# A decode-attention and FFN kernel: moving the FFN weight loads forward in the load stream, and reworking the last stage

## The chip, the cores and the metric

The kernel runs on one core of one Trainium2 chip. The metric is device microseconds per execution. A quoted time is the median of several runs; almost all runs of one kernel lie within 0.1% of that median. A profile is of one execution, whose span is some 2 us shorter than its measured time, because the span runs from the first to the last instruction. The program uses one core.

Engines: PE is TensorE (PEld its weight loads), DVE is VectorE, ACT is ScalarE, SP (SPq in the profile) is the sync engine, which issues nearly all loads.

## The reference

```python
x = A_x                                          # 2 x 1 x 512
q = layernorm(x) @ wq                            # 32 heads of 128, one query token per batch
scores = q k^T / sqrt(128)                       # k_cache: 2 x 32 x 8192 x 128, bf16
h  = x + (softmax(scores) @ v_cache) @ wo        # v_cache: the same size
y  = layernorm(h)
h2 = h + (relu(y @ W_gate) * (y @ W_up)) @ W_down   # 512 -> 1376 -> 512
```

Nearly all of the work is reading the two caches, 268 MB. A "pair" below is two heads of one batch: one K tile and one V tile of 4 MB each; there are 32 pairs. The weights wq, wo and the three FFN matrices are another 12.6 MB.

## The kernel before

Four buffers of 4 MB rotate: K of even pairs in 0, K of odd pairs in 2, V in 1 and 3. K[p+2] is issued when pair p has been read, V[p+2] when the P.V matmuls of pair p are done. VectorE computes three quarters of a pair's scores as a product and a tree of additions, in two halves; TensorE transposes and multiplies the rest:

```python
for c in range(NCH):                    # two halves, 48 of the 128 tiles each
    dve.wait(t_k[p])
    dve: prod = k_t[:, half, :] * q     # L324
    dve: four halving additions         # L332
    dve: scores = reduce(prod)          # L339
    if c == 0: ... TensorE: transposes and scores of the last 32 tiles; exp of those ...
    act: exp(scores)
    if last_pair and c == 0:
        t_O[3] = normalize(3, 24, 31, t_batch[3], False)   # pairs 24 to 30
```

At the end the FFN weights go into the buffer of K30, which has to be read first; the last V is issued after them, in four pieces:

```python
if p == NP - 2:                                   # pair 30
    sp.wait(*t_kfree[p])
    ... W_gate, W_up, W_down[0:1280] ("(r p) n -> p r n": rows of 1 KB) into slot[s] ...
    nc.sync.dma_start(wd_last[0:FR, :], B_W_down[1280:F]).then_inc(sem_w, 16)   # L384
...
if p == NP - 2:
    sp.wait(t_vlast)
    for ci, (j0, j1) in enumerate(((0, 48), (48, 96), (96, 112), (112, 128))):
        nc.sync.dma_start(slot[sl][:, ...], src[:, ...]).then_inc(sem_vl[ci], 16)   # L426
```

So the stream ends K30, V30, K31, weights, V31. Then come the output projection of the last pairs, the residual `hb`, and the FFN:

```python
pe.wait(t_O[3]); o_proj(range(24, 30), 0, 2); o_proj(range(30, 32), 0, 1)   # 32 matmuls
... o_scale; o_proj(range(30, 32), 1, 2) ...                                # 8 matmuls
hb = Wp + x
d_b = hb - mean;  d2 = d_b * d_b;  memset(Op[1]); memset(Sp[1])
t_u = ffn_in(Sp[1], wup);  t_g = ffn_in(Op[1], wgt)                  # 44 matmuls each
for c in range(DC): matmul(Sp[0][:, 64:66], lhsT=ones_f, rhs=d2[...])   # fp32 norm sums
hd = max(gate, 0) * up;  down projection (44 matmuls);  out = y * (1/var) + hb
```

The softmax here doesn't subtract the row's maximum and nothing guards it: scores larger than these inputs give would overflow.

## Time and profile before

Before: 683.12 us (682.39 to 683.75, 3 runs), span 680.7 us.

| What | Value | View |
|---|---|---|
| bytes moved | 281.97 MB | page, DMA queues |
| rate in most slices | 428 to 431 GB/s | page, slices |
| one pair on VectorE | 15.5 us | timeline, from K30's landing at 626.39 to 641.85 |
| K30 to K31 landing (8.4 MB) | 19.44 us | timeline |
| `hb` ready | 669.80 us | chain of waits |

The page's slices of the kernel before: one row per engine or quantity, 40 equal slices of 17 us, counted here from 0; the digits are tenths of busy time.

```profile
DVE  1777778867777887777782788776777886777781
DMA  9999999999999999999999999999999999999990
GB/s 374 437 432 431 428 428 430 430 429 430 432 429 431 430 429 429 430 430 429 430 345 435 429 428 428 428 430 431 428 429 430 429 429 430 430 429 430 409 360 27
```

The load engines are busy throughout, so the stream is the limit. VectorE is about three quarters busy: it keeps up, with idle time of about 4 us per pair. The dip to 345 (slice 20) is wo, in rows of 1 KB; the last three slices are the end of the stream.

The chain of waits of the kernel before, its end; columns are start, duration (us), and what it was.

```profile
639.48 11.62 SPq L384
651.10 0.05 issue
...
652.56 15.23 DMA slot<-in_A_v_cache_dram
667.79 0.05 issue
667.84 0.59 PE O L407 x16
668.42 1.35 PE W L303 x40
...
669.80 0.18 DVE hb L447
...
670.95 1.52 PE S L473 x44
672.47 1.39 PE O L473 x44
673.86 1.71 PE S L482 x8
675.56 1.47 PE O L501 x44
```

Here a load ends the stream: the last piece of V31 lands at 667.79, TensorE does 16 matmuls with it, then 40 of the output projection, then up, gate, the norm sums (L482, 8 records in fp32) and down, one after the other. The first line says that the sync engine was held for 11.62 us in issuing 96 rows of W_down; only then could the last V be issued. Stretches of 2 us at that place show a slower stream (the last two columns are DMA share and GB/s):

```profile
648.00:650.00 2.00, 2.00 (x31) 2.00 (x32) 1.97 (x2) 1.57 (x2) 0.00 (x0) 0.50 0.98 368
650.00:652.00 2.00, 1.07 (x19) 0.64 (x17) 1.94 (x2) 1.49 (x3) 0.00 (x0) 0.50 0.49 193
652.00:654.00 2.00, 0.00 (x0) 0.00 (x0) 1.86 (x6) 1.05 (x7) 0.00 (x0) 0.50 0.88 284
```

VectorE's two halves of pair 31 ended with this line in the timeline of the kernel before (start, duration, engine, line, operation), at 661.88, six microseconds before the last load landed:

```profile
661.33 0.55 DVE L339 TENSOR_REDUCE scores<-prod 128x48 f32<-128x384 bf16 x1
```

### The profile page before, as it was taken

To read this page: it belongs to the slowest core of one execution; us is meant where nothing else is said; L and a number is where in the kernel's file an instruction comes from. 1 tells how busy PE (TensorE), PEld (TensorE's weight loads), DVE (VectorE), ACT (ScalarE), POOL (GpSimd) and SP (SyncE) were. 2 spreads that over 40 slices of the span, in tenths; PEclk is the share of its full clock that TensorE was granted. 3 is DMA by queue.
4 is the path that set the end of the run, shared out by engine and by line. 5 is a ranking of instruction groups with operands and counts; after the bars stand their busy time and mean duration, and the time that the engine had idled before them with its cause. 6 is when DMAs were issued, how large, how long until landed. Compare 5 with 4: busy or idle time off the path is not lost.

```text
span 680.7 us, 14440 instructions
## 1 busy us (share of the span) xinstructions
PE 297.6 (44%) x6602; PEld 268.7 (39%) x6602; DVE 492.9 (72%) x426; ACT 202.6 (30%) x523; POOL 1.8 (0%) x11
## 2 busy tenths in 40 slices
PE   2544334444543445354342344535443444653436
PEld 2444334443433334344341333434433443543326
DVE  1777778867777887777782788776777886777781
ACT  0632223333222333332131233333222333332230
POOL 1000000000000000000000000000000000000000
PEclk9955566555555555655555556555556555555555
DMA  9999999999999999999999999999999999999990
GB/s 374 437 432 431 428 428 430 430 429 430 432 429 431 430 429 429 430 430 429 430 345 435 429 428 428 428 430 431 428 429 430 429 429 430 430 429 430 409 360 27
DMA packets 15936, 281.97 MB, mean 414 GB/s; under 512 B 1442, under 2 KB 6916, under 8 KB 7172
## 3 DMA queue, kind: packets, MB, share of 16 engines
q1 hardware_dynamic: 15872, 281.06, 97.1%
q8 instruction: 51, 0.84, 0.5%
q14 instruction: 9, 0.07, 0.0%
q10 hardware_dynamic: 4, 0.00, 0.0%
HBM read 281.05 MB, written 0.00 MB: 413 GB/s over the span
## 4 chain that ended last, share of the span: by engine, by line
DMA 69%; DVE 27%; SPq 2%; PE 1%; issue 1%; DVEq 0%
DMA slot<-in_A_k_cache_dram 66%; DVE prod L324 16%; DVE tb L332 6%; DVE prod L332 3%; DMA slot<-in_A_v_cache_dram 2%; SPq L384 2%; DVE scores L339 1%; PE S L482 0%; PE S L473 0%; PE O L501 0%; PE O L473 0%; PE W L303 0%; SPq L426 0%; SPq L133 0%; SPq L379 0%
## 5 line engine op out<-in xcount | busy, mean ns | idle before, releaser
L324 DVE TENSOR_TENSOR prod<-slot,q_b 128x6144 bf16<-128x6144 bf16 x64 | 214.9, 3358 | 135.3 <-DMA slot<-in_A_k_cache_dram 134.2
L407 PE MATMUL O<-e,slot 128*128 128x2 bf16 x4096 | 119.5, 165 | 248.4 <-ACT e L261 124.2
L407 PEld LDWEIGHTS O<-e,slot 128*128 128x128 bf16 x4096 | 114.4, 104 | 253.6 <-DMA slot<-in_A_v_cache_dram 126.9
L355 ACT ACTIVATE kT<-T 128x1024 bf16<-128x1024 bf16 x128 | 126.9, 1022 | 171.7 <-PE T L349 170.7
L349 PE MATMUL T<-ident,slot 128*128 128x128 bf16 x1024 | 123.6, 307 | 71.9 <-DMA slot<-in_A_k_cache_dram 71.9
L332 DVE TENSOR_TENSOR tb<-prod 128x3072 bf16<-128x3072 bf16 (+1 forms) x128 | 148.2, 1158 | 4.4
L349 PEld LDWEIGHTS T<-ident,slot 128*128 128x128 bf16 x1024 | 100.3, 141 | 74.9 <-DMA slot<-in_A_k_cache_dram 74.9
L261 ACT ACTIVATE e<-scores 64x48 bf16<-64x48 f32 x128 | 32.8, 256 | 255.0 <-DVE scores L339 253.4
L332 DVE TENSOR_TENSOR prod<-tb 128x1536 bf16<-128x1536 bf16 (+1 forms) x128 | 84.2, 658 | 4.4
L253 PE MATMUL S<-qT,kT 128*128 128x2 bf16 x1024 | 48.4, 168 | 33.0 <-ACT kT L355 31.7
L253 PEld LDWEIGHTS S<-qT,kT 128*128 128x128 bf16 x1024 | 41.1, 107 | 52.0 <-ACT kT L355 52.0
L339 DVE TENSOR_REDUCE scores<-prod 128x48 f32<-128x384 bf16 x64 | 35.4, 553 | 2.2
L261 ACT ACTIVATION_READ_ACCUMULATOR e<-scores 64x1 f32 x128 | 23.7, 185 | 0.0
L261 ACT ACTIVATE e<-S 64x32 bf16<-64x32 f32 x64 | 13.0, 204 | 15.1 <-PE S L253 14.3
L261 ACT ACTIVATION_READ_ACCUMULATOR e<-S 64x1 f32 x64 | 12.9, 201 | 0.7
L235 ACT ACTIVATE q_b<-O 128x512 bf16<-128x512 f32 x8 | 4.3, 594 | 15.6 <-PE O L230 15.6
L208 DVE CAST qT<-W 128x64 bf16<-128x64 f32 x1 | 0.2, 225 | 12.0 <-PE W L203 12.0
L203 PE MATMUL W<-xlT,slot 128*128 128x2 bf16 x128 | 3.6, 165 | 8.6 <-DMA slot<-in_A_wq_dram 8.6
L203 PEld LDWEIGHTS W<-xlT,slot 128*128 128x128 bf16 x128 | 3.5, 104 | 8.7 <-DMA slot<-in_A_wq_dram 8.7
L279 DVE TENSOR_REDUCE zr<-O 128x16 f32<-128x48 f32 (+1 forms) x4 | 0.8, 204 | 8.3 <-PE O L271 8.3
L271 PE MATMUL S<-zs,ones_f 128*128 128x6 f32 x2 | 0.6, 367 | 10.9 <-ACT e L261 10.9
L230 PE MATMUL O<-ident,qrep 128*128 128x128 bf16 x32 | 4.3, 303 | 1.7 <-ACT q_b L235 0.9
(56 smaller groups left out, 47.2 us busy)
## 6 DMA issues: line engine op xcount, KB each, us to landing
slot<-in_A_k_cache_dram SPq DMA_DIRECT2D x32, 4096.0 KB, 27.9
slot<-in_A_v_cache_dram SPq DMA_DIRECT2D x31, 4096.0 KB, 32.1
slot<-in_A_wq_dram SPq DMA_DIRECT2D x1, 4096.0 KB, 12.3
wo_sb<-in_A_wo_dram SPq DMA_DIRECT2D x1, 4096.0 KB, 43.4
slot<-in_A_v_cache_dram SPq DMA_DIRECT2D x2, 1536.0 KB, 12.1
slot<-in_B_W_gate_dram SPq DMA_DIRECT2D x1, 1376.0 KB, 10.0
slot<-in_B_W_up_dram SPq DMA_DIRECT2D x1, 1376.0 KB, 13.2
slot<-in_B_W_down_dram SPq DMA_DIRECT2D x1, 1280.0 KB, 15.0
```

The lines of the kernel that those rows point to most:

```text
L203: i = nc.tensor.matmul(Wp[:, h * B:(h + 1) * B], lhsT=wq[:, c, h * Dh:(h + 1) * Dh], rhs=lT[:, c * B:(c + 1) * B], start=(c == 0), stop=(c ...
L230: i = nc.tensor.matmul(Op[m % 2][:, k * 128:(k + 1) * 128], lhsT=qrep[m % 2][:, k * 128:(k + 1) * 128], rhs=ident[:], start=True, stop=True)
L235: t_cp[m] = act.run(nc.scalar.activation(out=q_b[:, m * 512:(m + 1) * 512], in_=Op[m % 2][:], func=ACT.Copy))
L253: i = nc.tensor.matmul(Sp[p % 2][:, 2 * jj:2 * jj + 2], lhsT=kT[n % 3][:, k * 128:(k + 1) * 128], rhs=qT[:, 2 * p:2 * p + 2], start=True, ...
L261: t = act.run(nc.scalar.activation(out=e_t[p % 2][q, j0:j0 + nj, a], in_=src(q, a), func=ACT.Exp, scale=inv_sqrt_dh, accum_out=zs[q, 2 * p ...
L324: t_dm = dve.run(nc.vector.tensor_tensor(out=prod[:], in0=k_t[:, c * JC:(c + 1) * JC, :], in1=qv, op=ALU.mult))
L332: dve.run(nc.vector.tensor_tensor(out=o, in0=cur[:, :, 0:half], in1=cur[:, :, half:w], op=ALU.add))
L339: t_s = dve.run(nc.vector.tensor_reduce(out=sc[:], in_=cur, axis=AX.X, op=ALU.add))
L349: i = nc.tensor.transpose(Tp[n % 3][:, k * 128:(k + 1) * 128], k_t[:, j, :], ident[:])
L355: t_ev[n] = act.run(nc.scalar.activation(out=kT[n % 3][:], in_=Tp[n % 3][:], func=ACT.Copy))
L384: nc.sync.dma_start(wd_last[0:FR, :], B_W_down[1280:F]).then_inc(sem_w, 16)
L407: i = nc.tensor.matmul(Op[k % 2][:, col:col + 2], lhsT=v_t[:, j, :], rhs=e_t[p % 2][:, j, :], start=(nmm == 0), stop=(nmm == J - 1))
```

## The change

The intent: give the FFN weights a home that doesn't depend on K30 (the buffer of wq, then of wo), so that they can be loaded early; let the stream end in V alone; shorten the last stage. Cut to its core:

```diff
+        X = sb("X", [128, XW + FC * D], BF16)          # wq, then wo, then the FFN weights
+                t_v[1] = load(3, slot[3][:], kv(A_v_cache, 1))
                 sp.wait(t_q)
-                t_v[1] = load(3, slot[3][:], kv(A_v_cache, 1))
+                ... wo heads 0-23 into X, heads 24-31 into wo_t (before: wo behind pair 14) ...
@@ main loop
-                        if last_pair and c == 0:
-                            t_O[3] = normalize(3, 24, 31, t_batch[3], False)
...
+                    if p < NP - 2:
+                        pv(p)
+                        if p == W_AT:                               # W_AT = 24 (before: 27)
+                            t_om = pe.run(o_proj(range(0, HM), 0, 2))
+                        if p < NP - 4:
+                            load_v(p + 2)
+                        elif p == NP - 3:                           # K31 was issued just above
+                            load_v(p + 1)
+                            load_v(p + 2, vparts)                   # last piece 8 tiles, was 16
+                        if p == W_AT + 2:                           # pair 26
+                            sp.wait(t_om)
+                            ... W_gate, W_up, W_down into X ...
@@ after the loop
+                pv(NP - 2)
+                t_O[3] = normalize(3, 24, 31, t_batch[3], False)
                 pe.wait(t_O[3])
-                o_proj(range(24, 30), 0, 2)
+                o_proj(range(HM, 30), 0, 2)
                 o_proj(range(30, 32), 0, 1)
+                normalize(4, 31, 32, z_sum(4, 31, 32), True)
+                pv(NP - 1)
@@ FFN
-                ... d2, two memsets, then up, gate, four fp32 matmuls for the norm sums ...
+                t_u = ffn_in(Sp[1], wup, 0, FC)
+                t_g = (ffn_in(Op[1], wgt, 0, FH), ffn_in(Wp, wgt, FH, FC))
+                ... d2, its sum over c, split into two bf16 parts vh on VectorE ...
+                for k in range(2):
+                    i = nc.tensor.matmul(Sp[0][:, 64:64 + B], lhsT=onesn[:], rhs=vh[:, k * B:(k + 1) * B], ...)
+                ... down in two halves, each after its half of hd ...
```

The stream now ends: K28, V28, weights, K29, V29, K30, K31, V30, V31.

## The prediction

> **What bounds it now.** The load stream. The page's slice table shows the DMA busy 9 tenths in 39 of 40 slices at 428-431 GB/s; 281.97 MB at 430 is 656 us of the 680.7 us span. The Trainium skill ("DMA: Bandwidth & Descriptors", Specifications) gives 435 GB/s as the fabric ceiling; the trace agrees, so only losses can be won. The timeline by line shows wo running at about 335 GB/s (it costs some 3 us over full rate). At the end, the issue of the last 96 rows of W_down blocks the sync queue for 11.62 us (639.5 to 651.1), so the last V (651.1) starts late: the stretches 650-654 move 193 and 284 GB/s. The last V lands at 667.8; 12.9 us of tail follow.
>
> **The step that decides.** The change moves the weights ahead of K29, and K31 ahead of V30. Same bytes, so the stream still ends at 666-668. The blocking issue moves too: K29 queues behind W_down's rows as the last V did, so I expect the bubble again, near 604. But the stream's last three transfers are now K31, V30, V31, and VectorE becomes the tail. From the timeline: one pair costs VectorE 15.5 us, one 4 MB transfer takes 9.85 us. K30 landed at 626.4; with 4.2 MB of weights ahead (10.8 us at the measured rates, up to 12 with the bubble) it lands at 637-638.5. VectorE then does pairs 30 and 31 without a pause: 31.0 us, to 668-669.5. Before, pair 31 was done at 661.9.
>
> Everything after that is serial in the new order, since the batch-3 normalisation now sits behind pair 31 on VectorE and the last P.V behind z_sum on PE: normalise 0.75, 32 output-projection matmuls 1.15, z_sum 0.5, 128 P.V matmuls 3.66 (28.6 ns each), scale and the last 8 matmuls 0.8. So the residual (hb) is ready at about 675.0-676.6 instead of 669.8: +5.2 to +6.8 us. Halving the last chunk gains nothing; V31 has landed when PE asks.
>
> **Gains in the tail, on the path.** The fp32 norm matmuls (8 records, 1.71 us on the chain) become two bf16 ones of 0.2; they fill the wait for the product, and the down projection starts as soon as the gate ends: -1.5 us. The two memsets and the square leave the path: -0.3. Total -1.8.
>
> **Off the path.** wo moves from pair 14 to the start, same rows and rate; K2 lands some 12.5 us later and pair 18 when it did. It blocks the sync queue there, the stream staying full. 96 projection matmuls move from pair 27 to 24, under the loads.
>
> **Sum.** +6.0 - 1.8 is about +4: **687.0 us**, 8 in 10 between 683.0 and 691.0. Faster by over 2%: 0.01; within 2%: 0.97; slower by over 2%: 0.02.
>
> **What would show it.** Chain of waits: right, if it ends through VectorE's work on pair 31 (pairs 30 and 31 back to back), not a V load. Timeline: last P.V starts some 8 us later than the old 662.9, at about 670, with no wait for V; down projection right behind the gate. Sync queue: a long blocked issue at 566-604; wo's dip in slices 3-4 instead of 20.
>
> **What would make it wrong.** If the blocked issue leaves no bubble near 604, everything comes 1-2 us earlier (about 685). If the blocked queue starves the stream at the start, 1-3 us later.  A gain needs K30 to land by about 633, which I do not see.

## The result, and the profile after

The changed kernel takes 686.34 us (686.09 to 686.68, 4 runs), the kernel before 682.82 us in the same rounds. The ratio is 1.005, with a 95% interval of 1.0033 to 1.0067: slower by about 3.5 us. The profile is of the slowest of the four runs: its span is 684.9 us, 4.2 more (the other three: 684.3 to 684.6).

The page's slices of the changed kernel:

```profile
DVE  1774577768877767887767778876777787728792
DMA  9999999999999999999999999999999999999970
GB/s 379 429 419 391 428 426 432 433 430 428 430 427 432 427 430 435 430 433 433 428 427 430 426 430 427 433 430 429 430 430 425 434 434 428 392 384 429 427 323 3
```

The stream looks as before, with wo's dip now in slices 2 and 3 and the weights' in 34 and 35. The stream ends about a microsecond later: the last piece of V31 is issued at 637.75 and lands 31.2 us later, near 668.9 (667.79 before). (The last slices, 3 GB/s against 27, can't be compared: they begin at 667.8 and 663.7.) VectorE, however, has a hole (the 2 in slice 35) and then three slices at 8, 7 and 9.

The end of the chain of waits of the changed kernel (same columns):

```profile
603.45 34.68 DMA slot<-in_A_k_cache_dram
638.15 3.37 DVE prod L367
...
653.72 3.37 DVE prod L367
...
668.63 0.55 DVE scores L382
669.18 0.12 DVE zr L285
...
669.83 1.23 PE W L310 x32
671.06 0.43 PE S L277 x2
671.50 3.42 PE O L335 x128
...
675.69 0.18 DVE hb L452
...
676.52 1.53 PE S L473 x44
678.05 0.64 PE O L473 x24
678.69 0.75 PE W L473 x20
679.43 0.05 PE S L502 x2
679.49 1.48 PE O L514 x44
```

No V load stands in this chain; the last one landed over 2 us before the P.V matmuls of pair 31 began (671.35 in TensorE's timeline). K30 landed at 638.15; from there VectorE works without a pause on pairs 30 and 31 until 669.18, 7.3 us later than before. Then everything is in series: normalisation, 32 projection matmuls, the sums, all 128 P.V matmuls of pair 31, and `hb` at 675.69 instead of 669.80. From `hb` on, the new last stage is shorter: 5.4 us instead of 7.3 to the start of the output's computation.

The stretches around the weights in the changed kernel (DMA share and GB/s in the last two columns):

```profile
596.00:600.00 4.00, 1.77 (x67) 1.80 (x68) 3.93 (x3) 0.67 (x4) 0.00 (x0) 0.50 0.82 309
600.00:604.00 4.00, 0.50 (x19) 0.41 (x16) 3.66 (x5) 0.17 (x2) 0.00 (x0) 0.50 0.79 272
604.00:608.00 4.00, 1.44 (x48) 1.36 (x48) 0.00 (x0) 0.50 (x4) 0.00 (x0) 0.50 1.08 405
```

And the sync engine's own timeline, which shows the held issue (here it is K29's, for 22.24 us):

```profile
568.52 0.43 SPq L432 DMA_DIRECT2D X<-in_B_W_down_dram  x1
569.00 0.62 SPq L435 DMA_DIRECT2D X<-in_B_W_down_dram  x1
580.04 22.24 SPq L136 DMA_DIRECT2D slot<-in_A_k_cache_dram  x1
```

### The profile page after: what moved, and what is told of

It is laid out like the page before. It is cut to its first block, busy times and chain, and to the rows that moved or that the text cites. A ratio compares the mean times of both kernels' runs of the same rounds, so it can differ in the third digit from the quotient of the medians.

```text
span 684.9 us, 14429 instructions
## 1 busy us (share of the span) xinstructions
PE 294.9 (43%) x6596; PEld 267.0 (39%) x6596; DVE 493.6 (72%) x428; ACT 202.3 (30%) x523; POOL 1.7 (0%) x11
## 4 chain that ended last, share of the span: by engine, by line
DMA 68%; DVE 30%; PE 1%; issue 1%; SPq 0%; DVEq 0%
DMA slot<-in_A_k_cache_dram 68%; DVE prod L367 17%; DVE tb L375 7%; DVE prod L375 4%; DVE scores L382 2%; PE O L335 0%; PE W L310 0%; PE S L473 0%; PE O L514 0%; SPq L136 0%; PE W L473 0%; PE O L473 0%; PE S L277 0%; SPq L152 0%; DVE O_sb L297 0%
## 5 line engine op out<-in xcount | busy, mean ns | idle before, releaser
L207 PE MATMUL W<-xlT,X 128*128 128x2 bf16 x128 | 3.6, 165 | 8.6 <-DMA X<-in_A_wq_dram 8.6
L207 PEld LDWEIGHTS W<-xlT,X 128*128 128x128 bf16 x128 | 3.5, 104 | 8.7 <-DMA X<-in_A_wq_dram 8.7
L236 PE MATMUL O<-ident,tb 128*128 128x128 bf16 x32 | 4.3, 302 | 1.7 <-ACT q_b L241 0.9
L310 PE MATMUL W<-O_sb,wo_t 128*128 128x2 bf16 (+1 forms) x40 | 1.7, 173 | 7.0 <-DVE O_sb L297 7.0
## 6 DMA issues: line engine op xcount, KB each, us to landing
X<-in_B_W_gate_dram SPq DMA_DIRECT2D x1, 1376.0 KB, 30.4
```

Of the source, the lines that this page charges most:

```text
L207: i = nc.tensor.matmul(Wp[:, h * B:(h + 1) * B], lhsT=wq[:, c, h * Dh:(h + 1) * Dh], rhs=lT[:, c * B:(c + 1) * B], start=(c == 0), stop=(c ...
L236: i = nc.tensor.matmul(Op[m % 2][:, k * 128:(k + 1) * 128], lhsT=qrep[m % 2][:, k * 128:(k + 1) * 128], rhs=ident[:], start=True, stop=True)
L310: i = nc.tensor.matmul(Wp[:, c * B + b0:c * B + b1], lhsT=wo_m[:, h, c, :] if h < HM else wo_l[:, h - HM, c, :], rhs=Ov[:, h // 2, h % 2, ...
```

## The experiments

The theory: the weights ahead of K29 push K30 back by the time of 4.2 MB, and since VectorE needs 31 us for the last two pairs, VectorE and not the stream becomes the tail. Rivals: (1) the order of K31 and V30 is to blame; (2) the serial order of the work after pair 31 is the whole cost; (3) the dip near 600 us; (4) wo at the start of the stream. Each run (the first row apart) was timed in five rounds against the kernel before (`before` in the table) on the same chip.

| Run | Median us | Before, same rounds | Ratio (95%) | Span |
|---|---|---|---|---|
| changed kernel | 686.34 | 682.82 | 1.005 (1.0033-1.0067) | 684.9 |
| w_last | 678.10 | 682.83 | 0.993 (0.9918-0.9943) | 676.2 |
| swap_kv | 690.12 | 682.83 | 1.0107 (1.0093-1.012) | 688.1 |
| tail_order | 683.98 | 682.83 | 1.0015 (1.0003-1.0028) | 682.1 |
| down_rows | 688.08 | 682.83 | 1.0078 (1.0064-1.0092) | 686.2 |
| before_ffn | 680.77 | 683.13 | 0.9965 (0.9952-0.9977) | 679.0 |
| wo_mid | 685.85 | 683.13 | 1.0037 (1.0025-1.005) | 683.9 |
| old_chunk | 686.42 | 683.13 | 1.0046 (1.0033-1.0058) | 684.4 |
| best | 674.34 | 683.13 | 0.9871 (0.9856-0.9886) | 672.3 |
| down_dma_only | 685.91 | 683.13 | 1.0039 (1.0026-1.0051) | 684.3 |
| after_again (the changed kernel again) | 686.37 | 683.13 | 1.0046 (1.0032-1.0059) | 684.3 |
| best2 | 675.15 | 683.13 | 0.9881 (0.9868-0.9895) | 673.7 |

### w_last: the weights behind the last V

```diff
-                        if p == W_AT + 2:
+                        if p == NP - 3:          # after load_v(p + 2, vparts)
```

> The changed kernel with one edit: the four FFN weight loads are issued after the last V instead of behind pair 26. Theory (the weights ahead of K29 push K30 back by 11.7 us, and the 31 us of VectorE work on pairs 30 and 31 then end after the loads): K30 lands near 627 instead of 638.2, VectorE ends pair 31 near 658 instead of 669.2, the weights land last near 667.5 and the gate and up products start there; span near 676, so about 8.5 us less than the changed kernel and 5 less than the kernel before. Rival (the cost is the serial order of the tail alone, whatever the stream order): the time from the last load to the end stays as it was and the total changes by less than 2 us. Second rival (the bubble near 600 us is the cost): only its 1.7 us come back.

Measured: 678.10 us, 8.2 less than the changed kernel, with a span of 676.2. In VectorE's timeline K30 is there at 626.69 and pair 31 ends at 657.7:

```profile
626.69 3.36 DVE L367 TENSOR_TENSOR prod<-slot,q_b 128x6144 bf16<-128x6144 bf16 x1 [3.95 <-DMA slot<-in_A_k_cache_dram]
...
657.17 0.55 DVE L382 TENSOR_REDUCE scores<-prod 128x48 f32<-128x384 bf16 x1
```

`hb` is ready at 664.23. TensorE's timeline then shows the wait for the weights:

```profile
664.45 0.27 PE L455 MATMUL S<-hb,onesn 128*128 128x2 bf16 x4 [0.26 <-DVE hb L452]
667.45 1.55 PE L473 MATMUL S<-d_b,X 128*128 128x2 bf16 x44 [2.73 <-DMA X<-in_B_W_down_dram]
```

The brackets give the idle time before an instruction and what ended it: 2.73 us for the weights, which land last. The serial order after pair 31 is untouched in this run, so rival 2 cannot be the whole cost; one moved line takes the loss away and more. The theory holds, to about a microsecond in each of its steps.

### swap_kv: V30 ahead of K31

```diff
-                        if p < NP - 4:
+                        if p < NP - 3:
                             load_v(p + 2)
                         elif p == NP - 3:
-                            load_v(p + 1)
                             load_v(p + 2, vparts)
```

> The changed kernel with one edit: V30 is issued ahead of K31, as in the kernel before; the weights stay behind pair 26. Theory (VectorE on pair 31 is the tail): K31 lands one transfer later, near 658, VectorE idles from 653.7 to 658 and ends pair 31 near 673.5, total 4 us slower than the changed kernel. Rival (moving K31 ahead of V30 is what cost the time): faster than the changed kernel, near the kernel before.

Measured: 690.12 us, 3.8 more than the changed kernel. VectorE's timeline has the start of pair 31:

```profile
657.00 3.36 DVE L367 TENSOR_TENSOR prod<-slot,q_b 128x6144 bf16<-128x6144 bf16 x1 [3.96 <-DMA slot<-in_A_k_cache_dram]
```

VectorE waits 3.96 us for K31. K30 came 0.6 us earlier than in the changed kernel's trace, so pair 31 ends 3.3 us later (672.46 against 669.18), and the spans differ by 3.2: the wait is the difference. Rival 1 falls: moving K31 ahead of V30 helped the changed kernel. It was the weights' place that hurt.

### tail_order: the work after pair 31 in another order

```diff
                     for c in range(NCH):
+                        if p == NP - 1 and c == 1:
+                            pv(NP - 2)
...                          # after the first product of that half
+                        if p == NP - 1 and c == 1:
+                            t_O[3] = normalize(3, 24, 31, t_batch[3], False)
@@ P.V of pair 31: parts 0, 2, 3 first, then z_sum, then part 1 (which needs the last exp)
```

> The changed kernel with the order after pair 31 mended: the batch-3 normalisation runs in the middle of pair 31 on VectorE, the 32 output-projection matmuls and three of the four parts of the last P.V (80 of 128 matmuls) run ahead of the last exp. Theory: those 1.2 and 2.3 us leave the path after VectorE, while VectorE's own end moves by 0.1 at most; about 2.4 us less than the changed kernel. Rival (the last V load, not VectorE, decides when the tail starts): no change.

Measured: 683.98 us, 2.4 less than the changed kernel. In TensorE's timeline, the projection and 80 of the P.V matmuls have moved in front of the last exp:

```profile
665.05 1.23 PE L310 MATMUL W<-O_sb,wo_t 128*128 128x2 bf16 x32 [2.32 <-DVE O_sb L297]
666.14 2.27 PE L338 MATMUL O<-e,slot 128*128 128x2 bf16 x80
670.13 0.59 PE L277 MATMUL S<-zs,ones_f 128*128 128x6 f32 x2 [1.72 <-ACT e L267]
670.58 1.42 PE L338 MATMUL O<-e,slot 128*128 128x2 bf16 x48
```

So of the cost, 2.4 us was the order of the work behind VectorE; the V loads were not what it waited for (the wait before z_sum is for ACT's exp).

### down_rows and down_dma_only: was it the dip near 600 us?

In down_rows, W_down comes in 10 KB rows per partition, and gate and up take their columns with a step of 10 so that the features match. In down_dma_only only the load is altered; the features then don't match, so its result is wrong.

```diff
-        B_W_down[0:1280].rearrange("(r p) n -> p r n", p=128)
+        B_W_down[0:1280].rearrange("(p r) n -> p (r n)", r=10)
-        lhsT=w[:, c, f * 128:f * 128 + fw]                                         # down_rows only
+        lhsT=w[:, :, 0:1280].rearrange("p c (q r) -> p c r q", r=10)[:, c, f, :]   # f < 10
```

> The changed kernel with W_down read as 10 KB rows per partition (feature p*10+r on partition p), the gate and up columns taken with a step of 10 to match. Theory of the bubble (1 KB rows run at 335 instead of 430 GB/s and hold up the next issue, so 596-604 moves 240-309 GB/s): the long blocked issue of K29 (22.2 us) goes, the stream gains about 2.5 us (0.9 from the rate, 1.7 from the bubble), all of it reaches the end. Rival (the bubble comes from something else, as the many weight queue entries or the strided products cost as much): no change or slower.

> The changed kernel with W_down read in 10 KB rows, the products left as they are (the result is wrong on purpose: the features do not match). It parts the two effects of the down_rows run. If the rows and the blocked issue cost the stream the 2.5 us forecast, this is 2.5 us less than the changed kernel; if, as the landings of K30 in down_rows say (637.2 against 638.2), they cost only 0.4 to 0.9, it is that much less, and the rest of down_rows was the products with a step of 10 (2.5 us more on TensorE).

Measured: down_rows 688.08 us, 1.7 more than the changed kernel instead of 2.5 less; down_dma_only 685.91 us, 0.5 less than after_again (the changed kernel timed again, with 686.3 expected and 686.37 measured), with intervals that overlap. The held issue did go (K29's issue took 0.34 us), and so did the dip; down_dma_only in stretches:

```profile
596.00:600.00 4.00, 1.69 (x64) 1.72 (x65) 3.93 (x3) 0.67 (x4) 0.00 (x0) 0.50 1.01 405
600.00:604.00 4.00, 0.58 (x22) 0.49 (x19) 3.64 (x5) 0.18 (x2) 0.00 (x0) 0.50 1.04 424
...
628.00:632.00 4.00, 2.27 (x80) 2.22 (x80) 3.93 (x3) 0.00 (x0) 0.00 (x0) 0.50 0.77 295
```

But another dip, to 295 GB/s, stands at 628 to 632, which the changed kernel doesn't have, and K30 landed at 637.70, between the changed kernel's 638.15 and after_again's 637.46. What the first dip cost is read from VectorE's timeline, where K29 arrives in the changed kernel and then in down_dma_only:

```profile
618.71 3.36 DVE L367 TENSOR_TENSOR prod<-slot,q_b 128x6144 bf16<-128x6144 bf16 x1 [14.91 <-DMA slot<-in_A_k_cache_dram]
```

```profile
618.32 3.36 DVE L367 TENSOR_TENSOR prod<-slot,q_b 128x6144 bf16<-128x6144 bf16 x1 [14.54 <-DMA slot<-in_A_k_cache_dram]
```

K28 had arrived at 588.34 and 588.32, so K29 came 30.4 us behind it with the dip and 30.0 without (30.4 in after_again, whose K28 came at 587.65; 30.0 in down_rows). From K29 to K30 it is 19.4 us in all four: the second dip delayed nothing. A visible dip is thus not yet a loss: what counts is when the next K lands. Rival 3 is worth about 0.4 us. That after_again's K30 is nevertheless the earlier one comes from a difference of 0.7 us that was there at K28; landings of K two pairs apart vary between 38.8 and 40.4 us in the undisturbed middle of all these kernels. Why the second dip appears is open.

What down_rows lost is on TensorE: from `hb` to the start of the output's computation it takes 7.9 us (674.77 to 682.68), where the changed kernel and down_dma_only take 5.4. Groups by form in the last microseconds of the changed kernel and then of down_rows (line, engine, operation, shapes, count | busy us, mean ns):

```profile
L473 PEld LDWEIGHTS S<-d_b,X 128*128 128x128 bf16 x40 | 1.2, 104 | 0.4 <-issue 0.4
```

```profile
L478 PEld LDWEIGHTS S<-d_b,X 128*128 128x128 bf16 x40 | 2.4, 156 | 0.4 <-issue 0.4
```

A weight load with a step of 10 elements takes 156 ns instead of 104, and the up product's 40 loads are busy for twice as long. The Trainium skill ("SBUF — State Buffer", section "Door 1: The DMA port swizzle", the note on cachelines) says that SBUF has lines of 16 bytes and that each access that crosses to a new line pays; a step of 10 bf16 elements leaves the line at every element, and this trace agrees with the direction. It does not prove the mechanism.

### before_ffn: the kernel before with the new last stage only

```diff
-                ... fp32 norm sums, memsets, gate and down whole ...
+                ... the changed kernel's last stage, word for word (W_down's last rows still in wd_last) ...
```

> The kernel before with only the change's last stage: norm sums as two bf16 parts instead of fp32, no memsets, gate and down in two halves. Theory: from the residual (hb) to the issue of the output takes 5.8 us instead of 7.7, so about 1.9 us less than the kernel before. Rival (this stage hides behind something else): no change.

Measured: 680.77 us, 2.4 less than before (span 1.7 less; 1.9 was forecast). This part of the change is a gain by itself. So the full 3.5 us of loss are a gain of about 2 and a cost of about 6 in the rest of the change. And w_last, which keeps all of that rest but the weights' place (96 projection matmuls at pair 24 included, which no run of their own tests), gains more than this run, 4.7 us over the kernel before: taken together, the other parts are not the loss.

### wo_mid and old_chunk: two parts that should not matter

```diff
-                ... wo loads after sp.wait(t_q) ...                          # wo_mid:
+                        if p == 14: ... the same two loads ...
-                vparts = (..., (0, 96, 120), (0, 120, 128))                   # old_chunk:
+                vparts = (..., (0, 96, 112), (0, 112, 128))
```

> The changed kernel with wo loaded behind pair 14, as in the kernel before, instead of at the start. Theory (the place of wo in the stream does not matter, its rows and rate are the same): within 0.7 us of the changed kernel. Rival (the blocked queue from 17 to 57 us, or wo at the start, starves the stream): 1 to 3 us less than the changed kernel.

> The changed kernel with the last V chunk at its old size (16 tiles instead of 8). Theory (all of V31 has landed some 3 us before the last P.V starts): no change, within 0.4 us. Rival (the last chunk's landing is waited for): 0.3 us or more slower.

Measured: wo_mid 685.85 us, 0.5 less than the changed kernel and within what was expected for "does not matter"; old_chunk 686.42 us, no change. Rival 4 falls, up to half a microsecond. In the trace of the changed kernel the second wo issue is held from 17.2 to 56.8 us, and K2 lands at 75.44 instead of 62.87; K17, the first K behind wo in the kernel before, then reaches VectorE about a microsecond apart in the two (370.56 before, 371.55 after), and so does K18 (390.00, 390.98).

### best and best2: a version that beats both

If the stream must end in something, let it be what the least work hangs on. In `best` the weights come last, in the order up, gate, down (in two pieces), each with its own semaphore, together with the order of tail_order:

```diff
-                        if p == W_AT + 2:
+                        if p == NP - 3:
                             sp.wait(t_om)
+                            ... W_up (sem_w), W_gate (sem_wf[0]) ...
+                            for k, (r0, r1) in enumerate(((0, FH), (FH, 10))):
+                                ... W_down rows r0*128 to r1*128 ....then_inc(sem_wf[1 + k], 16)
+                            ... the last 96 rows ....then_inc(sem_wf[3], 16)
-                pe.wait((sem_w, 64), t_d)
+                pe.wait((sem_w, 16), t_d)        # and one wait ahead of gate and of each half of down
```

> The changed kernel with the weights last in the stream (up, gate, down in two pieces, each with a semaphore of its own) and the order of the tail_order run. Theory: the last byte is then waited for by the second half of the down projection alone; hb near 662, up and gate done near 666, the down pieces land near 667, span near 673, 2 to 4 us less than the w_last run and 8 less than the kernel before. Rival (the weights' landing is later when they come last, or the whole tail follows the last landing anyway): as the w_last run, near 676.

> The best run with the last 96 rows of W_down loaded behind pair 26 instead of last. In the best run their issue was blocked for 6.8 us and they landed last (667.6). If that block delays the end, 0.3 to 1 us less than best (674.3); if the rows of the second piece decide, no change.

Measured: best 674.34 us, 12.0 less than the changed kernel and 1.3% less than the kernel before. TensorE's timeline at the end:

```profile
662.59 1.53 PE L481 MATMUL S<-d_b,X 128*128 128x2 bf16 x44 [0.34 <-DVE d_b L467]
...
667.62 0.80 PE L524 MATMUL O<-hd,X 128*128 128x2 bf16 x20 [0.48 <-DMA X<-in_B_W_down_dram]
```

Up and gate are done by 665.7, and only the 20 matmuls of the second half of down follow the last landing. (The wait of the first half is named VectorE's in the profile, but its piece of W_down landed at about 666.0 and fits better.) best2 loads the last 96 rows of W_down behind pair 26: 675.15 us, no gain. Its K29 landed at 608.48 instead of 607.27 (0.5 us of that were there at K28), and that lag remains to the end. From there to the landing of the piece that the last 20 matmuls wait for (667.49 in best, 668.77 in best2) it is 60.2 us in best and 60.3 in best2, so the held issue of those rows was not what set the end.

The runs were compared with the reference and passed, down_dma_only too, whose FFN features don't match. That comparison is thus not sharp for the FFN; that the FFN of best is right rests on its products being the changed kernel's own, with other waits; no measured result shows it.

## Why the prediction was right or wrong

The prediction was 687.0 us (683.0 to 691.0); the measured time is 686.34. The steps, from the chains shown above:

| Step | Predicted | Measured |
|---|---|---|
| K30 lands | 637 to 638.5 us | 638.15 (637.49 in after_again) |
| VectorE on pairs 30 and 31 | 31.0 us, to 668-669.5 | 31.03, to 669.18 |
| normalise, 32 matmuls, z_sum | 0.75, 1.15, 0.5 us | 0.65, 1.23, 0.43 |
| P.V; then scale and 8 matmuls | 3.66; 0.8 us | 3.46; 0.73 |
| `hb` ready | 675.0 to 676.6 us (+5.2 to +6.8) | 675.69 (+5.89) |
| last stage | -1.8 us | -1.96 in the chain; -2.4 in before_ffn |
| last P.V starts, without a wait for V | about 670 us | 671.35 |
| wo at the start, last piece halved | 0 | wo_mid -0.5, old_chunk 0 |

- The deciding step was right, and w_last and swap_kv show it rather than only fit it: moving the weights back takes 8.2 us away, and delaying K31 further adds 3.8 us.
- The serial order behind pair 31 was right; tail_order takes 2.4 us of it away.
- The dip near 604 was forecast and appeared at 596 to 604, but its price was mis-sized. The prediction held that everything comes 1 to 2 us earlier without it; down_dma_only, without it, is only 0.5 us faster, within the noise, and by the landings of K29 the dip is worth 0.4. The range for K30 was wide enough to hold both cases, so that K30 fell into it says nothing for the price of the dip. The held issue itself was forecast at 566 to 604; it is K29's, 580.04 to 602.28, while the last 96 rows of W_down, held in the kernel before, took 0.62 us.
- wo was said to cost "some 3 us over full rate", from stretches at 331 to 385 GB/s. By the landings it is less: in the kernel before V16 landed at 349.3 and wo at 360.8, 11.5 us for 4.19 MB, where the 4 MB tiles around it take 9.7; that is 1.8 us more.
- The stream was said to end at 666 to 668 still; it ended near 668.9 (668.1 in after_again). Nothing waited for it.
- The size of the last stage's gain was a little low (1.8 against 2.0 to 2.4).

## What to carry to other kernels

When the load stream is the limit, the order of the loads decides what is left to do when it ends: put first what the slowest consumer needs (here K, 15.5 us of VectorE for 9.7 us of loading), and last what the least work hangs on (here W_down, with 20 matmuls behind it). Loading something "early" is no gain in itself; in a full stream it delays everything behind it by its own duration (here K29 came 30.4 us behind K28 instead of 19.4). And judge a dip in the rate by when the next consumer's data land, not by its depth.

## What the Trainium skill lacked or had wrong

- "DMA: Bandwidth & Descriptors", Specifications: its minimum for line rate is 512 B or more. That row alone would let one expect full rate for 1 KB rows. Here wo's 1 KB rows ran at 331 to 385 GB/s in stretches of 5 us where large rows ran at 428 to 431, and took 11.5 us for 4.19 MB by the landings instead of 9.7. How much of that is the row size and how much the held queue is not parted; for W_down, 10 KB rows without the held issue brought K29 0.4 us sooner.
- The same page, "Where 436 GB/s comes from", says that the HBM side (about 358) binds for loads from HBM. With one core running, this stream sustains 428 to 431 GB/s, in line with the page's own single-core measurement of 425.
- No page gives a duration for how long a transfer of many small rows holds up the next issues on its queue (it would belong to "Perfetto Trace Analysis"): 11.62, 22.24, 25.36 and 39.64 us here, behind W_down and wo, and 0.34 us behind the same W_down in 10 KB rows.
- "TensorE: Matmul & The Clock Gate", section "Weight-path perf modes", allows packed or strided columns for the fast weight load, without a price for the step. Here a 128x128 bf16 load took 104 ns with step 1, 117 ns with step 4 (down) and 156 ns with step 10.
- No page explains why landings of K two pairs apart, the same 16.8 MB each time, vary between 38.8 and 40.4 us. In the changed kernel's trace it is single transfers, at 145, 244, 352, 460 and 549 us, that land 11.3 us after the one before instead of 9.7; it stays open.
